# Three input tiles change their DMA queue and one weight transpose its place in the order of SyncE's queue

## The chip, the core and the metric

The kernel runs on one core of one Trainium2 chip. The metric is the time of one execution on the device in microseconds (us). Three runs of the kernel before gave 144.81, 144.90 and 145.29 us, so the time before is their median, 144.9 us. A separate execution was profiled; its own time was 145.19 us, and its span from the first to the last instruction 143.9 us.

## What is computed

The input x has 2048 rows (tokens) of 448 bf16 numbers. Every row is normalised (mean taken off, divided by the standard deviation), and two branches are computed from the normalised rows and added to x:

```python
xn = _layernorm(x)                                   # [2048, 448]
qkv = xn @ wqkv                                      # 16 heads of 28
phi = concat(softmax(p), softmax(-p))                # p = q @ w_phi and k @ w_phi, by head
o = (phi_q @ (phi_k.T @ v)) / (phi_q @ sum(phi_k))   # linear attention
return x + o @ wo + silu(xn @ w1) @ w2               # w1: 448x1792, w2: 1792x448
```

## The kernel before

The 2048 tokens are 16 tiles of 128. Each tile is normalised on VectorE (`ln_tile`, L705: statistics in `bn_stats` L708 and `bn_aggr` L709, the scale on ScalarE L712 and VectorE L714 for tiles 0 to 3 or on GpSimd for the others, the normalised copy L723) and then turned, so that the 448 columns lie on the partitions (`xnT`). Tiles 0 to 3 are turned by TensorE against an identity (L541, called `tr0a`, `tr0`, `tr1`, `tr2`, `tr3`) and copied out of PSUM by ScalarE (tiles 0 to 2, `ev...`) or VectorE (tile 3). Tiles 4 to 15 are turned by DMA, two tiles to a transposing DMA (`xnT_dma5` for tiles 4 and 5, `xnT_dma7` for 6 and 7, and so on; L631). The weight of q and k is folded with w_phi; for that it is turned by DMA too, in nine pieces (`wT_dma0` to `wT_dma8`, also L631). A weight fold is a group of small matmuls; the first, `f0`, reads pieces 4 to 8.

All DMAs of the head of the kernel stand in two queues. SyncE (SP) issues x tile 0, x tile 1, four loads of w1 (`w1_0`, `w1_0r`, `w1_512`, `w1_512r`), x tiles 4 to 7 (one load), the rest of w1, wv, x tiles 8 to 11, and then what the chain at L1072 says. ScalarE issues only the load of x tiles 2 and 3. GpSimd issues four small loads of w_phi.

```python
load_x(0, 1)                                          # L607
load_x(1, 2)                                          # L608
load_x(2, 4, "act")                                   # L609
```

TensorE first runs 39 matmuls on constants (L591), then this order, which is written out by hand at L1047 and after it in `PLAN` (L361); `00a` is a part of the first feed-forward block on tile 0, `01a` the same on tile 1:

```python
"tr0a tr0 tr1 00a 10a 00b 10b 01a 11a 01b 11b tr2 20 21 02a tr3 12a ..."
```

In `PLAN`, `av4@6` is the first half of the v block of tiles 4 and 5, `aF10@2` the first half of a feed-forward block on tiles 4 to 7, and `f0@6` the fold.

VectorE's order at the start is written out too (L1033): bnst0, bnag0, bnst1, rstd0, bnag1, xn0, rstd1, xn1, bnst2, bnag2, bnst3, rstd2, xn2, bnag3, rstd3, xn3, ev3. ScalarE's is at L1034: the load of x 2 and 3 (`x2`), a warm-up of the Sqrt table (`warm_act`), ve0, ve1, ev0a, ev0, ev1a, ve2, ev1, ve3, ev2a, ev2, and a warm-up of the Silu table.

What these lists leave open is ordered by a planner (`_Prog.schedule`, L228). It runs when the program is built, gives each operation a start time from written-in costs, and so fixes the order of the instructions of every engine. A DMA has a transfer time (`xfer`) and a time to landing (`lat`) in it. TensorE's whole order is given to it; the orders of VectorE, ScalarE, GpSimd and SyncE are its own wherever no chain binds them.

A DMA in these lists can wait on another operation: L1036 makes the load of x 2 and 3 wait on `ident` (L564), which GpSimd computes from `ones` (L563), and L1037 gives the planner its times.

Of the kernel before, what the change touches and what calls it, by code (L numbers as in the profile page):

```python
# [370 lines left out]
def bass_parallel_sum__linear_kernel_hedgehog__dense_activation_silu__prompt_kernel(  # L371
# [29 lines left out]
    def rows_of(a, t0, t1):  # L401
        for u0, u1 in TILES:
            if u0 <= t0 < u1:
                v = a[0][128 * u0:128 * u1, :].rearrange("(p t) d -> p t d", p=128)
                return v[:, t0 - u0:t1 - u0, :]
# [3 lines left out]
    with es:  # L409
        def sb(name, shape, dt):  # L410
            return es.enter_context(nc.sbuf_tensor(name, shape, dt))
# [60 lines left out]
        ident = sb("ident", [128, 128], BF16)  # L472
# [7 lines left out]
        warm_act = sb("warm_act", [128, 4], F32)  # L480
# [76 lines left out]
        def load(dst, src, name, eng="sp", lat=1700.0):  # L557
            n = 2
            for _, cnt in list(dst.ap):
                n *= cnt  # L560
            P.dma(lambda e: e.dma_start(out=dst, in_=src), n / 280.0, writes=[dst], name=name, eng=eng, lat=lat)  # L561
# [35 lines left out]
        def load_x(t0, t1, eng="sp"):  # L597
            load(x_sb[:, t0:t1, :], rows_of(A_x, t0, t1), f"x{t0}", eng, lat=1400.0)
# [6 lines left out]
            load_rows4(w1_sb[:, :, c0:c1], B_w1, c0, c1, f"w1_{c0}", eng)  # L605

        load_x(0, 1)  # L607
        load_x(1, 2)  # L608
        load_x(2, 4, "act")  # L609
        load(w1_sb[:, 0:2, 0:512], B_w1[0:256, 0:512].rearrange("(k p) f -> p k f", p=128), "w1_0")  # L610
        load(w1_sb[:, 2:4, 0:512], bass.AP(B_w1.tensor, B_w1.offset + 256 * FF, [[FF, 128], [64 * FF, 2], [1, 512]]), "w1_0r")
        load_w1(512, 768)
# [37 lines left out]
        def fold_loads():  # L650
            for i in (*range(4, NW), *range(4)):
                c = max(0, KP * i - 64)
                dma_t(wT(i), A_wqkv[:, c:c + 128], 450.0, f"wT_dma{i}", 1750.0 if i == 6 else 1290.0, lat=950.0, sbuf=False)
# [368 lines left out]
        def chain(names):  # L1022
            byname = {o.name: o for o in P.ops}
            for a, b in zip(names, names[1:]):
                byname[b].odeps.add(byname[a].id)
                byname[b].odeps -= byname[b].deps
# [4 lines left out]
        fold()  # L1031
        act(warm_act[:], ones_bf[:, 0:4], ACTF.Silu, 4, "silu_table", table="silu", okeys_w=["sq"])
        chain("bnst0 bnag0 bnst1 rstd0 bnag1 xn0 rstd1 xn1 bnst2 bnag2 bnst3 rstd2 xn2 bnag3 rstd3 xn3 ev3".split())  # L1033
        chain("x2 warm_act ve0 ve1 ev0a ev0 ev1a ve2 ev1 ve3 ev2a ev2 silu_table".split())  # L1034
        byname = {o.name: o for o in P.ops}
        byname["x2"].deps.add(byname["ident"].id)  # L1036
        byname["x2"].xfer, byname["x2"].lat = 0.0, 2800.0  # L1037
        fold_loads()

        chunk = [(fp, c) for c in range(NCH) for fp in range(FP)]  # L1040
# [28 lines left out]

        for t in range(8, NT):  # L1070
            ln_tile(t)
        chain("x8 wT_dma4 wT_dma5 wT_dma6 x12 wT_dma7 xnT_dma5 xnT_dma7 wT_dma8 xnT_dma9 xnT_dma11 xnT_dma13 xnT_dma15 wT_dma0 wT_dma1 wT_dma2 wT_dma3 w2 "  # L1072
              "wo0 wor0 wo1 wor1".split())
        memset(phq[:, :, :, KP:128], 0.0, 400, "phq0")
        for t in (0, NEK):
# [199 lines left out]
```

## Time and profile before

| what | value |
|---|---|
| median of three runs | 144.9 us (144.81 to 145.29) |
| profiled execution, its own time | 145.19 us |
| its span, first to last instruction | 143.9 us |
| TensorE busy | 140.4 us (98%) |
| VectorE, ScalarE, GpSimd busy | 90.3, 79.7, 75.3 us (63, 55, 52%) |
| granted TensorE clock, whole span | 1.000 |
| DMA moved | 17.59 MB, mean 122 GB/s |

Times in the views count from the start of the span. PE is TensorE, PEld its weight load, DVE VectorE, ACT ScalarE, POOL GpSimd, SP SyncE; a q behind an engine's name is its instruction queue, which issues DMAs. q1 and q10 are DMA queues: in the head of the kernel q1 holds what SyncE issues and q10 what ScalarE issues. In the timeline the columns are start, duration, engine, line, operation, tiles, count, and in brackets the idle time before it with what ended it. In the table of DMA issues the last two columns are the size and the time from issue to landing. Both x_sb and the tiles of w1 (which lie in a buffer called phT) are loaded by the helper at L561, so one line number stands for many loads.

### The profile page before, as it was taken

The page shows a single profiled execution, that of the slowest core. Times are in us where ns is not written, and L with a number is a line of the kernel's source. Part 1 is how long each engine was busy: PE and PEld are TensorE (multiplying, and loading weights), DVE is VectorE, ACT ScalarE, POOL GpSimd, SP SyncE. Part 2 cuts the span into 40 slices and gives each one's busy share as a digit, 9 for nine tenths or more (in the row PEclk, how much of TensorE's full clock was granted, in tenths as well). Part 3 has the DMA queues.
Part 4 walks back from the last instruction along what each step waited for, and adds up shares of the span by engine and source line. Part 5 has one row for each costly group of instructions (what it writes and reads, how often), then busy time and mean ns, then how long its engine had stood idle before and what let it go on. Part 6 is the DMA issues. An engine that isn't in the chain of part 4 may idle for free.

```text
span 143.9 us, 4560 instructions
## 1 busy us (share of the span) xinstructions
PE 140.4 (98%) x1969; PEld 83.1 (58%) x1969; DVE 90.3 (63%) x194; ACT 79.7 (55%) x98; POOL 75.3 (52%) x95
## 2 busy tenths in 40 slices
PE   7799999999999999999999999999999999999994
PEld 7794444445444544477677656555555556555773
DVE  1879897700760069939049999957977564265533
ACT  4577866479996999889787949237440000000000
POOL 8808667430196008799944999993495700000000
PEclk9999999999999999999999999999999999999999
DMA  4999999555990000000000058959789998825422
GB/s 129 315 324 300 270 191 97 100 106 82 322 328 8 0 2 5 0 0 5 0 5 5 0 98 168 143 110 108 152 158 146 234 214 151 141 40 112 162 95 64
DMA packets 45044, 17.59 MB, mean 122 GB/s; under 512 B 36944, under 2 KB 44640, under 8 KB 45024
## 3 DMA queue, kind: packets, MB, share of 16 engines
q1 hardware_dynamic: 42448, 15.25, 53.3%
q10 hardware_dynamic: 2448, 2.02, 5.0%
q8 instruction: 15, 0.25, 0.7%
q0 software_dynamic: 128, 0.03, 0.1%
q14 instruction: 5, 0.04, 0.1%
HBM read 6.57 MB, written 1.84 MB: 58 GB/s over the span
## 4 chain that ended last, share of the span: by engine, by line
PE 94%; DMA 2%; DVE 1%; SPq 0%; ACT 0%; issue 0%
PE psum L524 94%; DMA x_sb<-in_A_x_dram 2%; PE psum L541 1%; DVE st L708 0%; SPq L561 0%; DVE RA L723 0%; DVE x_sb L1009 0%; ACT ve L712 0%; DVE rstd L714 0%; DVE mv L709 0%
## 5 line engine op out<-in xcount | busy, mean ns | idle before, releaser
L524 PE MATMUL psum<-xnT,phT 64*128 64x512 bf16 (+1 forms) x428 | 46.6, 350 | 0.0
L524 PE MATMUL psum<-w_sb,hT 64*128 64x448 bf16 (+4 forms) x455 | 46.0, 341 | 0.0
L843 DVE TENSOR_REDUCE Rec<-Ek_sb 128x32 f32<-128x896 bf16 (+1 forms) x20 | 24.6, 1257 | 18.6 <-ACT Ek_sb L547 18.6
L524 PEld LDWEIGHTS psum<-w_sb,hT 64*128 64x128 bf16 (+1 forms) x455 | 23.8, 94 | 17.2 <-issue 0.2
L547 ACT ACTIVATE hT<-psum 128x1024 bf16<-128x1024 f32 x28 | 27.6, 1024 | 10.8 <-PE psum L524 10.8
L524 PEld LDWEIGHTS psum<-xnT,phT 64*128 64x128 bf16 (+1 forms) x428 | 22.6, 95 | 17.6 <-ACT vaug L547 0.7
L880 POOL TENSOR_TENSOR RA<-Ek_sb,Rec 128x896 bf16<-128x896 bf16 x16 | 27.0, 1723 | 6.0 <-DVE Rec L844 4.4
L524 PE MATMUL psum<-Wqk,xnT 64*128 64x432 bf16 x224 | 24.4, 343 | 0.0
L547 ACT ACTIVATE Ek_sb<-psum 128x864 bf16<-128x864 f32 x24 | 20.4, 916 | 6.4 <-PE psum L524 5.5
L853 POOL TENSOR_TENSOR Ek_sb<-Ek_sb,Rec 128x896 bf16<-128x896 bf16 x8 | 13.4, 1698 | 16.3 <-DVE Rec L844 16.3
L524 PEld LDWEIGHTS psum<-Wqk,xnT 64*128 64x128 bf16 x224 | 11.1, 94 | 8.2 <-ACT hT L547 0.4
L547 ACT ACT_TABLE_LOAD x11 | 14.1, 1283 | 2.7 <-POOL Wp L554 1.8
L853 POOL TENSOR_TENSOR phT<-phT,Rec 128x896 bf16<-128x896 bf16 x8 | 13.4, 1699 | 1.7 <-issue 0.9
L524 PE MATMUL psum<-wv,xnT 64*128 64x448 bf16 x112 | 12.4, 349 | 0.0
L708 DVE BATCH_NORM_STATS2 st<-x_sb 128x6 f32<-128x448 bf16 x16 | 9.7, 604 | 3.5 <-DMA x_sb<-in_A_x_dram 3.5
L524 PE MATMUL psum<-wo_sb,vaug 64*128 64x448 bf16 (+2 forms) x102 | 11.3, 338 | 0.0
L1009 DVE TENSOR_TENSOR x_sb<-psum,x_sb 128x448 bf16<-128x448 f32 (+2 forms) x13 | 7.2, 583 | 5.5 <-PE psum L524 5.5
L988 DVE TENSOR_TENSOR vaug<-psum,rden 128x448 bf16<-128x448 f32 x16 | 9.3, 620 | 0.0
L723 DVE TENSOR_SCALAR RA<-x_sb,mv,rstd 128x384 bf16<-128x384 bf16 (+2 forms) x28 | 8.8, 352 | 0.8 <-POOL rstd L719 0.6
L843 DVE TENSOR_REDUCE Rec<-phT 128x64 f32<-128x1792 bf16 x4 | 8.0, 1990 | 1.9 <-ACT phT L547 1.8
L844 DVE RECIPROCAL Rec<-Rec 128x32 f32<-128x32 f32 (+1 forms) x24 | 8.8, 396 | 0.2
L547 ACT ACTIVATE vaug<-psum 128x896 bf16<-128x896 f32 x8 | 7.5, 949 | 2.4 <-PE psum L524 2.4
(60 smaller groups left out, 106.6 us busy)
## 6 DMA issues: line engine op xcount, KB each, us to landing
out_dram<-x_sb ACTq DMA_DIRECT2D x15, 112.0 KB, 2.4
w_sb<-in_B_w_dram SPq DMA_DIRECT2D x1, 1568.0 KB, 7.8
x_sb<-in_A_x_dram SPq DMA_DIRECT2D x3, 448.0 KB, 5.6
wo_sb<-in_A_wo_dram SPq DMA_DIRECT2D x2, 336.0 KB, 7.4
phT<-in_B_w_dram SPq DMA_DIRECT2D x3, 192.0 KB, 5.0
phT<-in_B_w_dram SPq DMA_DIRECT2D x1, 576.0 KB, 6.3
phT<-in_B_w_dram SPq DMA_DIRECT2D x2, 256.0 KB, 3.8
wv<-in_A_wqkv_dram SPq DMA_DIRECT2D x1, 336.0 KB, 6.7
```

The source lines that it names most:

```text
L524: r = e.matmul(dst, lhsT, rhs, start=st, stop=sp, skip_group_check=True)
L541: r = e.transpose(dst, src, ident[:])
L547: P.op("act", d_act(n), lambda e: e.activation(dst, src, func, scale=scale), reads=[src], writes=[dst], table=table, name=name, **keys)
L708: P.op("dve", 590, lambda e: e.bn_stats(st6[:, t, :], xs), reads=[xs], writes=[st6[:, t, :]], name=f"bnst{t}", okeys_w=["ln"])
L723: P.op("dve", dur, lambda e: e.tensor_scalar(dst, x_sb[:, t, c0:c1], mv[:, t, 0:1], rstd[:, t:t + 1], ALU.subtract, ALU.mult), reads=[xs, ...
L843: P.op("dve", 50 + 967 * n, lambda e: e.tensor_reduce(R2, E4, AXL.X, ALU.add), reads=[E4], writes=[R2], name=f"Ssum_{tag}")
L844: P.op("dve", 135 + 210 * n, lambda e: e.reciprocal(R2, R2), reads=[R2], writes=[R2], name="Rrec")
L853: P.op("pool", 1700, lambda e: e.tensor_tensor(E3, E3, Rk[:, :, None].broadcast_to([128, 32, DH]), ALU.mult), reads=[E3, Rk], writes=[E3], ...
L880: P.op("pool", 1700, lambda e: e.tensor_tensor(dst, Eq, Rq.rearrange("p (c j) -> p c j", c=CC)[:, :, :, None].broadcast_to([128, CC, 4, DH ...
L988: P.op("dve", 620, lambda e: e.tensor_tensor(o4, U4[:, :, :, 0:DH], rden4[:, :, :, None].broadcast_to([128, CC, 2, DH]), ALU.mult), reads= ...
L1009: P.op("dve", d_dve(cs.stop - cs.start), lambda e: e.tensor_tensor(res[:, cs], ob, addend[:, cs], ALU.add), reads=[ob, addend[:, cs]], wri ...
```

## The change

x tile 1 is loaded from ScalarE's queue, and x tiles 2 and 3 from SyncE's, second there, in the place of tile 1. In ScalarE's chain `x1` takes the place of `x2`. It waits on `ones`, where `x2` waited on `ident`, and the planner's figure for its landing is 2000 where it was 2800. On SyncE, `wT_dma7` moves from ahead of `xnT_dma5` and `xnT_dma7` to behind them. Sizes, numbers of DMAs and all arithmetic are the same.

```diff
         load_x(0, 1)
-        load_x(1, 2)
-        load_x(2, 4, "act")
+        load_x(1, 2, "act")
+        load_x(2, 4)
...
-        chain("x2 warm_act ve0 ve1 ev0a ev0 ev1a ve2 ev1 ve3 ev2a ev2 silu_table".split())
+        chain("x1 warm_act ve0 ve1 ev0a ev0 ev1a ve2 ev1 ve3 ev2a ev2 silu_table".split())
         byname = {o.name: o for o in P.ops}
-        byname["x2"].deps.add(byname["ident"].id)
-        byname["x2"].xfer, byname["x2"].lat = 0.0, 2800.0
+        byname["x1"].deps.add(byname["ones"].id)
+        byname["x1"].xfer, byname["x1"].lat = 0.0, 2000.0
...
-        chain("x8 wT_dma4 wT_dma5 wT_dma6 x12 wT_dma7 xnT_dma5 xnT_dma7 wT_dma8 xnT_dma9 xnT_dma11 xnT_dma13 xnT_dma15 wT_dma0 wT_dma1 wT_dma2 wT_dma3 w2 "
+        chain("x8 wT_dma4 wT_dma5 wT_dma6 x12 xnT_dma5 xnT_dma7 wT_dma7 wT_dma8 xnT_dma9 xnT_dma11 xnT_dma13 xnT_dma15 wT_dma0 wT_dma1 wT_dma2 wT_dma3 w2 "
               "wo0 wor0 wo1 wor1".split())
```

## The prediction

> **What bounds the kernel now.** I read the busy shares first, then the chain that ended last in order of time, then the timeline of the first 10 us, then the DMA views for the same stretch.
>
> ```profile
> PE 140.4 (98%) x1969; PEld 83.1 (58%) x1969; DVE 90.3 (63%) x194; ACT 79.7 (55%) x98; POOL 75.3 (52%) x95
> ```
>
> ```profile
> 1.28 3.00 DMA x_sb<-in_A_x_dram
> ...
> 4.30 0.63 DVE st L708
> ...
> 5.70 0.41 DVE RA L723
> ...
> 6.16 0.40 PE psum L541 x4
> 6.55 1.35 PE psum L524 x24
> 7.90 0.01 issue
> ...
> 9.43 132.57 PE psum L524 x1849
> ```
>
> The second fence is the chain (start, duration, what). From 6.16 to 142.00 it never leaves TensorE. The engine's own waits over the whole span say the same: PE waited on another engine for 0.7 us in all, twice, both for VectorE's normalised copy, ahead of tr0 (5.48) and tr1 (6.16). So what counts is when tr1 starts, and then whether TensorE is still never kept waiting. Its start hangs on a DMA: x tile 1, issued on SyncE at 1.28 and landed at 4.28, 3.00 us later.
>
> ```profile
> 2.90 0.63 DVE L708 BATCH_NORM_STATS2 st<-x_sb 128x6 f32<-128x448 bf16 x1 [2.90 <-DMA x_sb<-in_A_x_dram]
> 3.56 0.18 DVE L709 BATCH_NORM_AGGREGATE mv<-st 128x2 f32<-128x6 f32 x1
> 4.30 0.63 DVE L708 BATCH_NORM_STATS2 st<-x_sb 128x6 f32<-128x448 bf16 x1 [0.56 <-DMA x_sb<-in_A_x_dram]
> ```
>
> This is VectorE's timeline: tile 0's statistics, their aggregate, and tile 1's statistics after 0.56 us of idling for x tile 1. That idle time is all the change can win at the head of the kernel.
>
> ```profile
> x_sb<-in_A_x_dram SPq DMA_DIRECT2D x1, 112.0 KB, 2.1
> x_sb<-in_A_x_dram SPq DMA_DIRECT2D x1, 112.0 KB, 3.0
> x_sb<-in_A_x_dram ACTq DMA_DIRECT2D x1, 224.0 KB, 3.1
> ```
>
> These are the DMA issues of x tile 0, x tile 1 and x tiles 2 and 3 (from the windows about 0.8, 1.3 and 1.4 us). Tile 1 has the size of tile 0 and takes 0.9 us longer. The DMA queues say why, in the window 3.00 to 3.25:
>
> ```profile
> q10 hardware_dynamic: 45, 0.08, 97.1%
> q1 hardware_dynamic: 6, 0.00, 5.3%
> ```
>
> In that quarter of a microsecond ScalarE's queue moved 45 packets of x 2 and 3 and SyncE's 6. (In the window before, 2.75 to 3.00, it was 24 against 66.) So tile 1 is all but done by 3.0; its last few packets then crawl beside the other queue until 4.28.
>
> **The change part by part.** All of it is set against the profiled execution (span 143.9, own time 145.19), which ran 0.29 above the median of 144.9; I put the difference on the median. A change under 0.3%, 0.43 us, is about what a measurement of this kernel cannot tell from none.
>
> *x tile 1 on ScalarE.* ScalarE's load was issued at 1.41, 0.03 after `ident` ended (1.09 + 0.29 = 1.38). `ones` ends at 0.80 + 0.20 = 1.00, so x 1 is issued at 1.03, 0.25 earlier than on SyncE. Its way to landing from that queue is not in the trace. From below it is bounded by the row of the same size with nothing beside it, 2.1 us (landing 3.13), from above by ScalarE's row of twice the size, 3.1 us (4.13). The same sharing that the two queues showed gives a middle: x 2 and 3, issued at 1.41, moved first in the window 2.75 to 3.00, so 1.2 to 1.3 us after issue; x 1 should move from about 2.3, while x 2 and 3 follow x 0 on SyncE. Until 2.5 the queues had moved 31 + 97 kB (63 and 195 GB/s for 0.5 us each), that is x 0 (115 kB) and a little. If x 1 then has half of some 340 GB/s, its 115 kB need 0.7 us, to about 3.2; x 0's own landing at 2.88 lies 0.4 behind its last full window, so 3.6. I take 3.7, as the last of the transfers' parts have been the late ones, and keep 3.13 and 4.13.
>
> *x tile 0 beside it.* x 0 now has company from 2.3 on. Between nothing and half of the rate for its last 0.2 us, its landing moves by 0 to 0.2; I take 0.1, so tile 0's statistics start at 3.00.
>
> *The sum at the head.* VectorE is free for tile 1's statistics 0.76 after those of tile 0 began (2.90, 3.56, and 0.10 from an aggregate to the next instruction, as at 4.96 and 5.06). So they start at the later of 3.72 and 3.76: 3.76, where it was 4.30. That is 0.54 earlier; by the bounds, between 0.17 (4.13) and 0.64 (3.66, x 0 unmoved). All that follows on VectorE and ScalarE is a chain off that instruction. Only tr0 meets something fixed: the 39 constant matmuls end at 0.84 + 4.19 = 5.03, and 5.48 - 0.54 would be 4.94. The 0.09 delays ScalarE's copies of tile 0 and, behind them in its queue, ve2 of tile 2; I count 0.04. Net: **0.50 us**.
>
> *x 2 and 3 second on SyncE.* Same issue time as x 1 had (1.28), and the next issue stays at 1.74: ScalarE's issue took 0.38, SyncE's 0.41. They may land as late as 5.4 (tile 2's statistics ran at 6.02) before anyone waits; they landed at 4.5 and would now by about 4.3. The bytes ahead of w1_0 are the same 448 KB on both queues together. ScalarE's queue is free 0.38 earlier, which nobody needs: it idled 0.46 ahead of ve0.
>
> *Loads that do not move with the head.* They are issued by the clock of SyncE's queue. w1_0r (issued 2.21, 4.0 to landing: 6.2) is first read by the ninth matmul after tr1, at 6.39 + 8 x 0.056 = 6.84, then 6.34: 0.1 left, and the 0.18 us that PEld idles ahead of tr2 (7.91) is cover behind it. x 4 to 7 (3.77 + 4.6 = 8.4) is read at 9.81, then 9.3. x 8 to 11 (7.41 + 7.6 = 15.0) is read at 15.37, then 14.9: VectorE waits 0.1 there, far ahead of TensorE. None costs anything.
>
> *wT_dma7 behind xnT_dma5 and 7.* The transposes' places on SyncE and in TensorE's weight loads are these:
>
> ```profile
> 13.44 1.32 SPq L631 DMA_TRANSPOSE Y_sb<-in_A_wqkv_dram  x1
> 14.81 3.00 SPq L631 DMA_TRANSPOSE xnT<-RA  x2
> 17.85 1.26 SPq L631 DMA_TRANSPOSE Y_sb<-in_A_wqkv_dram  x1
> ```
>
> ```profile
> 20.88 0.50 PEld L524 LDWEIGHTS psum<-xnT,phT 64*128 64x128 bf16 x6
> ...
> 23.77 0.36 PEld L524 LDWEIGHTS psum<-BD,Y_sb 64*128 64x128 bf16 x7
> ```
>
> xnT_dma7 was issued at 16.16 and landed 4.1 later, 20.2; aF10 reads it at 20.88. With the head 0.50 earlier and this edit left out, 0.2 us would be left. With it xnT_dma5 is issued at 13.44 (tile 5's copy, over at 13.50, is then over at 13.0) and xnT_dma7 once tile 7's copy is done (14.70 + 0.76 - 0.5 = 15.0), both 1.2 to 1.4 earlier, so that 1.4 or more is left. Behind them wT_dma7 is issued about 16.3 to 16.6 and wT_dma8 in its old place, 17.85, landing 3.1 later at 21.0. The fold reads both at 23.3: 2.3 left, and that is this part's price if its cover goes. Cost and gain: nothing, beyond keeping the 0.50.
>
> The sum is 144.9 - 0.50 = **144.4**; the span would read 143.4.
>
> By the Trainium skill (DMA: Bandwidth & Descriptors, section "Issuing engines are not separate DMA queues") loads issued by several engines run on the same 16 DMA engines and interleave, and issuing from another engine saves only the time of the issue. By that rule this change would save 0.25 us and no more; the sum would be 144.65. The trace agrees in part: the 45 packets against 6 are interleaving, but they also show that it is the neighbour, and not the issue, that made tile 1 late.
>
> **Rivals.** *Only the issue is saved.* x 1 keeps its 3.0 us whatever its queue, since the same 448 KB are moved in the same time: landing 1.03 + 3.0 = 4.03, statistics at 4.05, gain 0.25, time **144.65**. For it: 3.0 and 3.1 are alike for two loads that overlapped. Against: 2.1 for x 0, and 66 packets against 24 for the load that started first.
>
> *x 1 is served last.* SyncE's queue holds x 0 and x 2, 3 back to back and keeps the DMA engines. All 448 KB (459 kB) were moved by about 3.6 (31, 97, 41, 92, 85, 87 kB in the windows to 3.50); with the tail of x 1 before, over a microsecond, it lands at 4.3 to 4.6. Time 144.9 to 145.2; I take **144.95**.
>
> *The planner's new order costs more than the head wins* (the other side). The planner gets other landing times and orders VectorE, ScalarE, GpSimd and SyncE anew. The place is ScalarE from 20 to 60 us, where its copies out of PSUM release TensorE with little to spare: PEld waited for ScalarE's hT and vaug seven times, 1.8 us, 0.4 at most, hidden by matmuls still running. If one copy of hT (1.02) is put ahead of the one that TensorE needs, it stalls by about 1.02 - 0.4 = 0.6; if a table load (1.28) comes with it, by 1.9. From a stall of 0.93 on the kernel is slower by over 0.3%; at 1.4 it takes **145.8**. Against it: most of these copies are released by TensorE, whose order is given. The change also cannot fail to do what it says: x 1's wait on the landing is the one on the chain.
>
> **How the numbers follow.** Forecast, a gain of 0.35 to 0.64 (144.25 to 144.55; most of it over 0.43): 0.52. Only the issue: 0.18. x 1 last: 0.10. Planner: 0.20, a few of these within 0.3%. Faster by over 0.3%: 0.50 (some of the forecast's lower end falls out, some planner luck comes in). Within: 0.31, slower: 0.19. The predicted time is 144.4. The range goes from 144.15 (the full 0.64 and 0.1 of better order) to 145.4, which leaves out most of the planner's case and a little at the lower end.
>
> **What would show it.** In the profile of the changed kernel: ScalarE's load of 112 KB issued at about 1.03 and landed by 3.7; tile 1's statistics near 3.76 with little or no idling ahead of them; tr1 near 5.66; the chain on TensorE from there with 132.6 us in one piece; xnT_dma5 issued near 13.4. Wrong if tile 1's statistics still wait beyond 4.1, if tile 0's move beyond 3.1, or if PE shows waits after 12 us that it did not have.

## The result: slower by a third of a percent

Over 22 runs of each kernel the change took 145.52 us (median) against 144.96 before; the ratio is 1.0033 with a 95% interval of 1.0018 to 1.0049, taken without one run of the changed kernel (147.52) that fell in a slower state. The forecast was 144.4. The profiled execution of the changed kernel took 145.47 us, with a span of 144.2.

The chain that ended last, in the changed kernel (start, duration, what):

```profile
1.27 0.41 SPq L561
...
1.73 0.43 SPq L561
2.16 0.04 issue
2.20 5.11 DMA phT<-in_B_w_dram
7.32 0.05 issue
7.36 1.07 PE psum L524 x16
8.43 0.22 PE psum L541 x4
8.65 0.89 PE psum L524 x16
9.55 0.22 PE psum L541 x4
9.77 132.52 PE psum L524 x1849
```

The wait for x tile 1 and VectorE's work on it are gone from its start. In their place stands one load into phT, issued at 2.20 and 5.11 us under way: w1_0r. From 9.77 on TensorE runs for 132.52 us in one piece, where it was 132.57 from 9.43; so between these two executions all of the difference arises in the first 10 us. The timeline there, of VectorE and of TensorE and its weight loads:

```profile
3.60 0.59 DVE L708 BATCH_NORM_STATS2 st<-x_sb 128x6 f32<-128x448 bf16 x1
```

```profile
5.42 0.23 PEld L541 LDWEIGHTS psum<-ident,RA 128*128 128x128 bf16 x4 [0.24 <-DVE RA L723]
...
7.36 0.90 PEld L524 LDWEIGHTS psum<-xnT,phT 128*128 128x128 bf16 x16 [1.19 <-DMA phT<-in_B_w_dram]
7.36 1.07 PE L524 MATMUL psum<-xnT,phT 128*128 128x128 bf16 x16 [1.02 <-DMA phT<-in_B_w_dram]
```

Tile 1's statistics run at 3.60 with no idle time ahead (4.30 before), and tile 1 is turned from 5.42 on (6.16 before): the head is 0.7 us earlier. Then TensorE stands for 1.02 us, after its first eight matmuls, until w1_0r has landed. The DMA issues of x 1, w1_0r and x 4 to 7 in the changed kernel, and below them the last two in the kernel before (last columns: size, us to landing):

```profile
x_sb<-in_A_x_dram ACTq DMA_DIRECT2D x1, 112.0 KB, 2.0
phT<-in_B_w_dram SPq DMA_DIRECT2D x1, 256.0 KB, 5.1
x_sb<-in_A_x_dram SPq DMA_DIRECT2D x1, 448.0 KB, 6.1
```

```profile
phT<-in_B_w_dram SPq DMA_DIRECT2D x1, 256.0 KB, 4.0
x_sb<-in_A_x_dram SPq DMA_DIRECT2D x1, 448.0 KB, 4.6
```

x 1 gained a full microsecond on its way (2.0 against 3.0); w1_0r lost 1.1, and x 4 to 7 lost 1.5, though both were issued at the same time as before, after the same number of bytes. And on SyncE the transposes stand so:

```profile
13.30 0.58 SPq L561 DMA_DIRECT2D x_sb<-in_A_x_dram  x1
13.93 3.81 SPq L631 DMA_TRANSPOSE xnT<-RA  x2
17.78 2.56 SPq L631 DMA_TRANSPOSE Y_sb<-in_A_wqkv_dram  x2
```

The last line holds wT_dma7 and wT_dma8; the second of the two is issued at 19.1, not at 17.85. It needs 4.2 us, so it lands at 23.3. The fold began at 24.1 in this execution and did not wait.

### The profile page after: what moved, and what is told of

Same layout as the page of the kernel before. It is cut to its first block, busy times and chain, and to the rows that moved or that the text cites. A ratio compares the mean times of both kernels' runs of the same rounds, so it can differ in the third digit from the quotient of the medians.

```text
span 144.2 us, 4561 instructions
## 1 busy us (share of the span) xinstructions
PE 140.3 (97%) x1969; PEld 82.6 (57%) x1969; DVE 90.1 (63%) x194; ACT 79.6 (55%) x98; POOL 75.2 (52%) x95
## 4 chain that ended last, share of the span: by engine, by line
PE 94%; DMA 4%; SPq 1%; DVE 0%; issue 0%
PE psum L524 93%; DMA phT<-in_B_w_dram 4%; SPq L561 1%; PE psum L541 0%; DVE x_sb L1009 0%
## 5 line engine op out<-in xcount | busy, mean ns | idle before, releaser
L843 DVE TENSOR_REDUCE Rec<-Ek_sb 128x32 f32<-128x896 bf16 (+1 forms) x20 | 24.6, 1256 | 18.6 <-ACT Ek_sb L547 18.6
L547 ACT ACTIVATE hT<-psum 128x1024 bf16<-128x1024 f32 x28 | 27.6, 1024 | 10.9 <-PE psum L524 10.8
L524 PE MATMUL psum<-Wqk,xnT 64*128 64x432 bf16 x224 | 24.4, 343 | 0.0
L853 POOL TENSOR_TENSOR Ek_sb<-Ek_sb,Rec 128x896 bf16<-128x896 bf16 x8 | 13.4, 1698 | 16.3 <-DVE Rec L844 16.3
```

Source lines behind the costliest of these rows:

```text
L524: r = e.matmul(dst, lhsT, rhs, start=st, stop=sp, skip_group_check=True)
L547: P.op("act", d_act(n), lambda e: e.activation(dst, src, func, scale=scale), reads=[src], writes=[dst], table=table, name=name, **keys)
L843: P.op("dve", 50 + 967 * n, lambda e: e.tensor_reduce(R2, E4, AXL.X, ALU.add), reads=[E4], writes=[R2], name=f"Ssum_{tag}")
L853: P.op("pool", 1700, lambda e: e.tensor_tensor(E3, E3, Rk[:, :, None].broadcast_to([128, 32, DH]), ALU.mult), reads=[E3, Rk], writes=[E3], ...
```

## The experiments

Two theories stood at first. A: TensorE's new wait for w1_0r eats the gain. B: the transposes' new order costs the time. The first four kernels take each apart. Each ratio below is to the kernel before, run alongside.

**The head without w1_0r, on the changed kernel and on the one before (`after_no_w1r`, `before_no_w1r`).**

```diff
-            fns = pair_block(b0, 512, lambda i, kt, r: w1_sb[r, kt, (2 * fp + i) * 128:(2 * fp + i + 1) * 128],
+            fns = pair_block(b0, 512, lambda i, kt, r: w1_sb[r, kt - 2 if c == 0 and fp < 2 and kt > 1 else kt, (2 * fp + i) * 128:(2 * fp + i + 1) * 128],
```

> The changed kernel, but the first two feed-forward blocks of the head (tokens 0 to 511, 256 and 256 columns of w1) read rows 0 to 255 of w1 a second time in place of rows 256 to 447, so that nothing early reads the load w1_0r (the output is not the reference's there). Theory A (TensorE's wait of 1.0 us for w1_0r ate what the earlier x tile 1 won): no wait for that load; the tiles' chain of 5.4 to 9.1 us bounds again and the time falls 0.4 to 0.7 below the kernel before, to 144.3 to 144.5, unless the next loads of w1 take the place of the wait. Theory B (the transposes' new order on SyncE costs the time): no change against the changed kernel, 145.4. Theory C (one DMA engine paused by chance in the profiled execution): also below the changed kernel, by less than 0.3.

Measured: 145.59, ratio 1.0050 (1.0029 to 1.0071). Theory A alone had failed. The two waits of TensorE for others, in its profile (total, times, longest):

```profile
PE psum L524 <- ACT xnT L547: 0.4, 1, 0.4
PE psum L524 <- DMA Y_sb<-in_A_wqkv_dram: 0.4, 1, 0.4
```

The first is at the very first product of the head (6.23). The view names ScalarE's copy; w1_0, which the same instruction waits for, landed at 6.10 here. The second is the fold at 24.16, waiting for wT_dma8, which landed at 24.0.

> The kernel before with the same replacement of rows of w1 in the head. Theory A: in the kernel before w1_0r lands ahead of its use in most executions, so 0 to 0.2 us are won: 144.7 to 144.9, and less spread between executions. Theories B and C: the same as before, 144.9.

Measured: 144.86, ratio 0.9990 (0.9977 to 1.0003). In the kernel before w1_0r holds up little or nothing.

**Each part alone.** `head_only` is the changed kernel with the chain at L1072 of the kernel before, `wt_only` the kernel before with that chain of the changed one:

```diff
-        chain("x8 wT_dma4 wT_dma5 wT_dma6 x12 wT_dma7 xnT_dma5 xnT_dma7 wT_dma8 ...
+        chain("x8 wT_dma4 wT_dma5 wT_dma6 x12 xnT_dma5 xnT_dma7 wT_dma7 wT_dma8 ...
```

> The first part of the change alone: x tile 1 from ScalarE, x 2 and 3 second on SyncE; the transposes in their old order. Theory A: like the changed kernel, 145.3 to 145.6, with a wait of TensorE for w1_0r of 0.5 us or more. Theory B: 144.4, as the prediction's sum had it.

Measured: 145.12, ratio 1.0004 (0.9988 to 1.0021). Neither theory's number. The head was early (tile 1's statistics at 3.63), w1_0 landed at 5.9 and w1_0r at 6.7, and TensorE waited 0.8 us for loads of w1, 0.6 of it at 13.81, for columns 1024 to 1791:

```profile
13.81 0.39 PE L524 MATMUL psum<-xnT,phT 64*128 64x512 bf16 x2 [0.60 <-DMA phT<-in_B_w_dram]
```

So this part wins nothing and loses nothing that can be measured. In this execution, which was itself 0.5 above the kernel's median, what it won was waited out again at the loads that follow.

> The second part of the change alone: wT_dma7 behind xnT_dma5 and xnT_dma7, the loads of x as before. Theory A: no change against the kernel before, 144.9 within 0.2. Theory B: 145.3 to 145.5.

Measured: 145.39, ratio 1.0024 (1.0002 to 1.0046). The loss that theory B expected, from the part of the change that was to cost nothing. In its profile x 1 happened to land early (3.4) and TensorE waited for no load in the head. The fold, and wT_dma8's way to landing (issued 18.6):

```profile
24.42 0.18 PE L524 MATMUL psum<-BD,Y_sb 64*128 64x56 bf16 x1 [0.92 <-POOL rstd L719]
```

```profile
Y_sb<-in_A_wqkv_dram SPq DMA_TRANSPOSE x1, 5.7
```

The wait is put down to GpSimd's rstd, the last releaser that the view could find; what ended it is wT_dma8, at 18.6 + 5.7 = 24.3. Why 5.7 us for a transpose that took 3.1 before is seen in the busy times by stretch of the same kernel (last two columns: DMA share and GB/s):

```profile
21.50:22.00 0.50, 0.50 (x8) 0.24 (x6) 0.50 (x3) 0.00 (x0) 0.42 (x2) 1.00 3.15 135
22.00:22.50 0.50, 0.50 (x8) 0.22 (x6) 0.50 (x3) 0.47 (x1) 0.50 (x2) 1.00 0.19 11
22.50:23.00 0.50, 0.50 (x8) 0.26 (x6) 0.50 (x2) 0.47 (x1) 0.42 (x2) 1.00 0.08 9
23.00:23.50 0.50, 0.50 (x6) 0.00 (x1) 0.50 (x4) 0.00 (x0) 0.29 (x1) 1.00 3.31 193
```

From 22.0 to 23.0 the DMA engines all but stand still. In the kernel before the same happens from 23.0 to 24.0 (11 and 47 GB/s in its halves), and what is under way then is xnT_dma9, which landed 5.1 us after its issue at 19.15 and was not read for another seven. One place later in the queue, wT_dma8 is the one that is caught. The other profiles bear this out: in the seven with the new order wT_dma8 landed at 23.3 to 24.4, in the eleven with the old one at 20.9 to 22.9, and the fold began at 23.4 to 25.1.

Theory D came from this: two loads are too late for the earlier head, w1 and wT_dma8, and each alone can eat the gain. Theory E: all loads behind the head land later, so that some other load takes up any wait that is removed.

**Both waits taken away; and the fold's wait alone (`after_no_w1r_wt`, `wt_only_no_wt`).** The fold reads pieces 5 and 6 for 7 and 8:

```diff
-                        mms.append((banks[b][:, c:c + PW], wT(i)[rows, KS[kt]:KS[kt] + 128], rhs, b not in seen, n == len(jobs[side]) - 1))
+                        mms.append((banks[b][:, c:c + PW], wT(i - 2 if i > 6 else i)[rows, KS[kt]:KS[kt] + 128], rhs, b not in seen, n == len(jobs[side]) - 1))
```

> The changed kernel with two waits taken away by other data: the head does not read w1_0r (it reads rows 0 to 255 of w1 twice), and the fold reads pieces 5 and 6 of the turned weight in place of 7 and 8 (the output is not the reference's there). Theory D, formed from the runs so far: two loads now land too late for the earlier head, w1_0r for its first use and wT_dma8 for the fold, and each alone is enough to eat the gain; with both gone the kernel is faster than the one before by 0.3 to 0.6, 144.3 to 144.6. Theory E (every load behind the head lands later when x 2 and 3 stand in SyncE's queue, so that some other load takes the wait): TensorE shows another wait for a load, at the first use of columns 512 to 1791 of w1 or of the turned tiles 4 to 7, and the time stays within 0.3 of the kernel before or above.

Measured: 144.92, ratio 0.9995 (0.9978 to 1.0012). Against the same kernel with the fold's wait (`after_no_w1r`, 1.0050) this is 0.8 us, and the two intervals lie apart: the cost of the fold's wait for wT_dma8 is shown. But the 0.3 to 0.6 that D hoped for is not there. w1_0 landed at 6.3 and its first product ran at 6.44 (6.39 before), after a wait of 0.3, as E has it.

> The second part of the change alone (wT_dma7 behind xnT_dma5 and 7), with the fold reading pieces 5 and 6 in place of 7 and 8 (output not the reference's there). Theory D: the loss of the second part alone (ratio 1.0024) came from the fold's wait for wT_dma8, so it goes: 144.7 to 145.0. If the loss is elsewhere on SyncE or in the DMA engines, it stays at 145.2 to 145.5.

Measured: 144.88, ratio 1.0005 (0.9982 to 1.0027), from 1.0024 (1.0002 to 1.0046) with the wait; as expected, though the two intervals overlap.

**Other ways to an early head.** `both_act` adds x 2 and 3 to ScalarE's queue behind x 1, `head_w1r_act` adds w1_0r there; both have the old order of the transposes. The edits are shown against the changed kernel.

```diff
-        load_x(2, 4)
+        load_x(2, 4, "act")
...
-        chain("x1 warm_act ve0 ...
+        chain("x1 x2 warm_act ve0 ...
```

> x 1 and, behind it, x 2 and 3 all from ScalarE; SyncE goes from x 0 straight to w1, each of its issues 0.46 earlier; the transposes in the old order. Theory D: w1_0r lands about 0.4 earlier than in the changed kernel and wT_dma8 by 21, so most of the earlier head is kept: 144.3 to 144.6. Theory E, in its form that it is the large rows in SyncE's queue that make the later loads late: x 4 to 7 lands near 8.5 as in the kernel before, not near 9.8 as in the changed one. If instead x 1 on ScalarE makes them late, it lands near 9.8 here too and the time is 144.9 to 145.3.

Measured: 145.00, ratio 1.0011 (0.9995 to 1.0027). w1_0 landed at 4.8, but x 2 and 3 at 5.7; TensorE stood 0.2 us at 7.24 for a copy of tile 1 that ScalarE had queued behind its work on tile 2. x 4 to 7 landed at 9.2, 6.0 after its issue, so the large rows of x 2 and 3 in SyncE's queue are not what delays it.

```diff
-        load(w1_sb[:, 2:4, 0:512], ..., "w1_0r")
+        load(w1_sb[:, 2:4, 0:512], ..., "w1_0r", "act")
...
-        chain("x1 warm_act ve0 ...
+        chain("x1 w1_0r warm_act ve0 ...
```

> The first part of the change alone (old order of the transposes), with w1_0r moved to ScalarE's queue behind x 1, issued at 1.45 where it was 2.20. Theory D: w1_0r lands before 6.0, TensorE does not wait for it, and 0.3 to 0.6 are won: 144.3 to 144.6. Theory E: a later load of w1 takes the wait, as w1 columns 1024 to 1791 did in the run of the first part alone, and the time stays at 144.9 to 145.2.

Measured: 145.54, ratio 1.0041 (1.0023 to 1.0058). A miss for both theories: w1_0r landed at 6.3, w1_0 only at 6.8, and TensorE stood 0.9 us for it.

**The two kernels once more (`before_again`, `after_again`), and x from one queue (`all_sp`) or later (`before_x2_late`).**

> The kernel before, profiled once more. Theory F (its profiled execution had an unusually late x tile 1, so that the prediction's base was too high): x 1 lands 0.3 to 0.9 earlier than 4.28, the first transposes of tile 1 start before 6.0, and part of that is lost again to another wait or the span is shorter. If 4.28 is typical, x 1 lands at 4.1 to 4.4 and the chain is the same.

Measured: span 144.1, x 1 landed at 4.5. 4.28 was not unusual, as theory F would have it; but other profiles with the same start had 3.4 and 3.6 (`wt_only`, `wt_only_no_wt`), so with the same head x 1 varies by over a microsecond between executions.

```profile
4.50 0.63 DVE L708 BATCH_NORM_STATS2 st<-x_sb 128x6 f32<-128x448 bf16 x1 [0.80 <-DMA x_sb<-in_A_x_dram]
```

> The changed kernel, profiled once more. Theory D with E: tile 1's transposes start near 5.5 as before, TensorE then waits for w1_0 or w1_0r by 0.3 to 1.0, and, where that wait is small, for wT_dma8 at the fold near 24. If the wait for w1_0r in the first profile was a chance pause of one DMA engine, neither load keeps TensorE waiting and the span is 143.3 to 143.6.

Measured: span 145.1. Tile 1's statistics at 3.90; w1_0 landed at 7.1 and held TensorE for 1.07 us. So the first profile's wait for w1 was not a chance pause of one execution, though this execution, at 146.36, was itself 0.8 above the kernel's median.

```profile
7.25 0.93 PE L524 MATMUL psum<-xnT,phT 128*128 128x128 bf16 x9 [1.07 <-DMA phT<-in_B_w_dram]
```

The kernel before, with the load of x 2 and 3 on SyncE:

```diff
-        load_x(2, 4, "act")
+        load_x(2, 4)
```

> x 0, x 1, x 2 and 3 all from SyncE in this order; nothing from ScalarE; w1 is issued 0.46 later; the transposes in the old order. If it is the two queues at once that let some DMA engines fall behind in the changed kernel (x 4 to 7 landed at 9.2 to 9.9 in its kind, 8.4 to 8.8 in the other), x 4 to 7 lands near 8.6 here and the time is 144.7 to 145.0. If it is the large rows of x 2 and 3 ahead of w1 in SyncE's queue, x 4 to 7 lands near 9.7 and the time is 145.0 to 145.5.

Measured: 145.65, ratio 1.0065 (1.0032 to 1.0098); x 4 to 7 landed at 10.4, the latest of all, 6.2 after its issue (0.5 of the lateness is the later issue; this execution took 146.71, 1.1 above the kernel's median). "Two queues at once" is not needed for the lateness; with one queue alone it was no better.

The kernel before, with the load of x 2 and 3 held back:

```diff
-        byname["x2"].deps.add(byname["ident"].id)
+        byname["x2"].deps.add(byname["wp_zero"].id)
```

> The kernel before with the load of x 2 and 3 on ScalarE held back by one more wait: it waits on the clearing of Wp0 (over at 1.79) in place of ident (1.38), so it is issued 0.4 later. If its packets are what holds up the last of x 1, x 1 lands at 3.3 to 3.6 and the head starts 0.3 to 0.6 earlier; by theory E (w1 then bounds the head) no more than 0.2 of it is kept: 144.7 to 144.9. By the prediction's own sum 144.4.

Measured: 145.29, ratio 1.0025 (1.0008 to 1.0042), slower than either expectation. x 1 landed at 3.4, as the prediction's account of the late packets says it should (though `wt_only` had 3.4 without this), and TensorE waited 0.3 for w1_0 (6.3) instead.

**What makes w1 late (`after_x1_ident`, `before_x2_ones`).** Two kernels exchange the moment of ScalarE's load (1.04 or 1.41) between the two arrangements (the second does the opposite to `x2` of the kernel before):

```diff
-        byname["x1"].deps.add(byname["ones"].id)
+        byname["x1"].deps.add(byname["ident"].id)
```

> The changed kernel, x 1 on ScalarE waiting on ident again, so issued at 1.41 in place of 1.04. If w1 is late because x 1 on ScalarE starts beside x 0, w1_0 lands before 5.8 and x 4 to 7 before 8.9 here. If it is late because x 2 and 3 stand ahead of it in SyncE's queue (224 KB, where x 1 is 112), it lands at 5.8 to 7 as in the changed kernel and its kind, x 4 to 7 at 9.2 to 10, and the time stays at 145.2 to 145.8.

> The kernel before, x 2 and 3 on ScalarE waiting on ones, so issued at 1.04 in place of 1.41, beside x 0. If an early start on ScalarE's queue beside x 0 is what lets w1 fall behind, w1_0 lands at 5.8 to 7 and the time is 145.2 to 145.8. If it is what stands ahead of w1 in SyncE's queue, w1_0 lands at 5.2 to 5.7 as in the kernel before, x 1 somewhat later than there, and the time is 144.8 to 145.3.

The changed arrangement, issued at 1.41 (x 1, w1_0r, x 4 to 7):

```profile
x_sb<-in_A_x_dram ACTq DMA_DIRECT2D x1, 112.0 KB, 3.0
phT<-in_B_w_dram SPq DMA_DIRECT2D x1, 256.0 KB, 4.1
x_sb<-in_A_x_dram SPq DMA_DIRECT2D x1, 448.0 KB, 4.7
```

The old arrangement, issued at 1.04 (w1_0r, x 4 to 7, and the head's wait):

```profile
phT<-in_B_w_dram SPq DMA_DIRECT2D x1, 256.0 KB, 5.1
x_sb<-in_A_x_dram SPq DMA_DIRECT2D x1, 448.0 KB, 5.7
```

```profile
7.39 0.28 PE L524 MATMUL psum<-xnT,phT 128*128 128x128 bf16 x2 [0.50 <-DMA phT<-in_B_w_dram]
```

In these profiles it goes with the moment, not with the tile: issued at 1.41, x 1 takes 3.0 us even from ScalarE and w1 is early; issued at 1.04, w1_0r takes 5.1 us even in the old arrangement. Times: 1.0046 (1.0026 to 1.0067) and 1.0029 (1.0012 to 1.0047), so neither is a way out. The profiled execution of `after_x1_ident` took 145.26, 0.25 below its median, and shows no wait of TensorE for a load, so its loss of 0.46% is not explained by it. The landings (issue plus time to landing) of the profiles with one of the two arrangements, and of `all_sp`, in us:

| profile | ScalarE's load at | x 1 | w1_0 | w1_0r | x 4 to 7 |
|---|---|---|---|---|---|
| before | 1.4 | 4.3 | 5.4 | 6.2 | 8.4 |
| before_again | 1.4 | 4.5 | 5.3 | 6.1 | 8.6 |
| before_no_w1r | 1.4 | 4.1 | 5.7 | 6.5 | 8.8 |
| wt_only | 1.4 | 3.4 | 5.3 | 6.0 | 8.5 |
| wt_only_no_wt | 1.4 | 3.6 | 5.5 | 6.6 | 8.8 |
| after_x1_ident | 1.4 | 4.4 | 5.6 | 6.3 | 8.5 |
| head_x1_ident | 1.4 | 4.6 | 5.3 | 6.1 | 9.1 |
| before_x2_late | 1.8 | 3.4 | 6.3 | 6.9 | 9.1 |
| changed | 1.0 | 3.1 | 5.0 | 7.3 | 9.9 |
| after_again | 1.0 | 3.4 | 7.1 | 7.9 | 10.3 |
| after_no_w1r | 1.0 | 3.1 | 6.1 | 6.9 | 9.8 |
| after_no_w1r_wt | 1.0 | 3.4 | 6.3 | 7.1 | 9.2 |
| head_only | 1.0 | 3.1 | 5.9 | 6.7 | 9.7 |
| before_x2_ones | 1.0 | 4.2 | 5.9 | 7.3 | 9.5 |
| all_sp | none | 3.4 | 5.2 | 7.3 | 10.4 |

One more kernel takes x 3 out of the load ahead of w1 (`head_x3_late`; the first part of the change alone):

```diff
-        load_x(2, 4)
+        load_x(2, 3)
...
-        load_w1(512, 768)
+        load_w1(512, 768); load_x(3, 4)
...
-            xs = x_sb[:, t, :]
+            xs = x_sb[:, 2 if t == 3 else t, :]
```

> The first part of the change alone (old order of the transposes), with x 3 taken out of the load ahead of w1: only x 2 (112 KB) stands there, x 3 is loaded behind w1_512, and tile 3 is normalised from the data of tile 2 (output not the reference's there). So 112 KB less stand ahead of w1_0 in SyncE's queue, as in the kernel before. If the bytes ahead of w1 in its queue are what keeps TensorE waiting, w1_0 lands by 5.6 and w1_0r by 6.4, TensorE waits for neither by more than 0.2, and the earlier head is kept: 144.3 to 144.7. If one DMA engine falls behind for another reason, the waits stay at 0.3 to 1 and the time at 144.9 to 145.3.

Measured: 145.57, ratio 1.0052 (1.0030 to 1.0073). That is above both expected ranges. With 112 KB less ahead of it w1_0 landed at 5.7 and w1_0r at 6.5, and neither held TensorE; but the next blocks of w1 did, at 11.5 and at 13.7. The transposes of tile 2 (tr2) ran 0.4 us earlier than in the kernel before (7.51, not 7.91), the fold 0.4 later. That is theory E once more.

The last kernel is `after_x1_ident` with the old order of the transposes.

> The first part of the change alone, x 1 on ScalarE waiting on ident (issued at 1.41), the transposes in the old order. The same head with the new order of the transposes was slower by 0.46% although w1 landed early in its profile. If that loss is wT_dma8 landing late for the fold, it is gone here: w1_0 before 5.8, wT_dma8 near 21, x 1 near 4.3, and the time is that of the kernel before, 144.8 to 145.1. If the loss is in the head, it stays at 145.3 to 145.6.

Measured: 145.38, ratio 1.0026 (0.9992 to 1.0061). wT_dma8 landed at 21.5, w1_0 at 5.3, x 1 at 4.6. The interval holds both answers, so how the 0.46% of `after_x1_ident` divides between the fold and the head stays open. No kernel tried is clearly faster than the one before.

## Why the prediction was wrong, by its own steps

**x tile 1 on ScalarE: right, and larger.** Issued at 1.04 (1.03 forecast), landed at 3.08 (3.7 taken, 3.13 the lower bound), statistics at 3.60 (3.76), tile 1 turned from 5.42 (5.66). x 0 was not delayed here: its statistics moved from 2.90 to 2.84 (3.14 in `after_again`). In these two profiles 0.24 was saved at the issue and 1.2 at the landing. Over all profiles x 1 landed at 3.1 to 3.4 in the eight that issue it at 1.04 from ScalarE, and at 3.4 to 4.5 in the five with the head of the kernel before, a mean gain of 0.7. So the rival "only the issue is saved" is out on the mean, and with it, as a figure for one load, the rule of the Trainium skill beside it (DMA: Bandwidth & Descriptors, section "Issuing engines are not separate DMA queues").

**Loads that do not move with the head: here it failed.** The step said "The bytes ahead of w1_0 are the same 448 KB on both queues together" and kept w1_0r's landing at 6.2, with 0.1 left. The bytes were the same and the landing was not: w1_0r landed at 7.3, and in six of the other eight profiles with the early issue w1_0, which TensorE needs first, landed at 5.9 to 7.1 (5.4 before). "0.1 left" from one profile was no cover, for TensorE reads w1 as soon as x 1 lets it. Before, x 1 and w1_0r were ready nearly together (the head read w1_0r at 6.84, 0.6 after it landed); winning 0.7 at one and losing 1.1 at the other made a loss of 0.3 in the profiled pair. Over the runs this part alone neither won nor lost (1.0004). The signs of being wrong that the prediction named for TensorE began at 12 us, behind the place where this wait stood (7.36).

**wT_dma7 behind xnT_dma5 and 7: failed.** The step put wT_dma8 "in its old place, 17.85, landing 3.1 later at 21.0", with 2.3 left. It was issued at 19.1 (18.6 with this part alone). xnT_dma5 went out at 13.9, and the two xnT transposes held SyncE's queue until 17.7, where the step had 16.3 to 16.6: xnT_dma7 waited for tile 7's copy until 15.8 (15.0 taken), and the two issues took 1.6 and 1.9 us (1.3 and 1.65 before). The load of x 12 to 15 ahead of them, issued at 13.3, is not the reason: it was issued at 13.3 in `before_again` too, and wT_dma8 went out at 17.8 there. Then the 3.1 us were wrong too, 4.2 to 5.7 in the seven profiles with this order, since the later place met the stretch in which the DMA engines nearly stood still. This part alone costs 0.24% (0.02 to 0.46), on these estimates most of the 0.33% that the whole change lost, and the fold's wait cost 0.8 us in the changed kernel that does not read w1_0r in the head.

**The base.** The step "I put the difference on the median" took x 1's landing of 4.28 for typical. It ranges from 3.4 to 4.5 in the five profiles with the head of the kernel before, so part of the idle time to be won was not there in every execution.

**The planner.** The orders of TensorE, VectorE and GpSimd are the same in both kernels, and ScalarE's but for its load; the rival for the slower side had the wrong place: the 0.19 for a slower kernel was given for a reason that did not occur. The right question, "whether TensorE is still never kept waiting", was in the text, and was answered from landings that the change itself moved.

## What to carry to other kernels

When the wait that starts the critical chain is shortened, list every load that the chain reads in the next microseconds and treat their landings as unknown again, above all if the edit touches the queues that bring them. A margin of 0.1 us read from one profile of a DMA is no margin; take two or three profiles first. Of a reordered queue, add up each entry anew, with waits and issue times, down to the last entry that anyone reads soon.

## What the runs showed of the hardware

The moment at which a second queue's first load was issued, 1.04 or 1.41 us, went with whether later loads of another queue landed early or late. x 4 to 7 took 4.6 to 5.3 us to landing in the seven profiles with 1.41 and 5.5 to 6.5 in the nine with 1.04, `both_act` (6.0) and `head_w1r_act` (5.7) among them. Issued later still, at 1.8, it was no gain (`before_x2_late`: w1_0 at 6.3, x 4 to 7 5.3 after its issue), and with one queue alone the same load took 6.2. Why a load issued 0.37 earlier, beside x 0, goes with loads issued a microsecond later falling behind was not found. The tile and the queue of x 2 and 3 were exchanged and are not it; 112 KB less ahead of w1 in SyncE's queue brought w1 0.2 earlier than in `head_only`, within what varies between executions.

From 22 to 23 us the DMA engines moved some 10 GB/s in `wt_only`. The traces of all eighteen profiles have such a stretch (under 30 GB/s for 0.5 to 1.3 us), and in each it begins 0.4 to 1.4 us after a 16 KB packet of the instruction queue q8 that starts between 21.2 and 24.0; the latest packet (`all_sp`, 23.97) has the latest stretch (24.4). That this packet, or that of q14 (the other instruction queue) near it, causes the stretch was not tried.
